# Layer 1's rational function from squares: ScalarE squares h, quotients of coefficients kept in registers, order table made anew

## The chip, the core and the metric

The kernel runs on one core of a Trainium2 chip. A core has five engines that run side by side, each through its own queue in order: TensorE (PE, matrix products into PSUM), VectorE (DVE), ScalarE (ACT), GpSimd (POOL) and SyncE (SP, which here only issues DMA transfers). The metric is the device time of one launch in microseconds. Three runs of the kernel before gave a median of 1600.95 us (1600.79 to 1603.09).

## What is computed

Attention with a packed set of 32 queries per head, then two layers over 4608 tokens of 512 features, each with 2048 hidden units. Cut to what matters:

```
p_packed = softmax(p k^T / 8) v                 # 8 batches x 8 heads, 32 packed rows, 576 positions
x = softmax(q p_packed^T / 8) p_packed          # 4608 x 512 after the heads are joined

h = x @ w_in                                    # layer 1
P = a[0] + a[1]*h + a[2]*h*h + a[3]*h*h*h
Q = 1 + |b[0]|*|h| + |b[1]|*h*h
x = (P / (Q + 1e-6)) @ w_out

h = x @ moe2_w_in                               # layer 2
out = (h * cos(h)) @ moe2_w_out
```

The weights are 64-bit numbers in memory; the kernel makes 32-bit ones of them on the chip. Each matrix product of the layers is made of three products of high and low parts.

## The kernel before

**Stages.** The attention works in 16 units (8 batches, two groups of four heads). A unit transposes k and q on PE in two pieces each (`trans`; ACT copies the piece out of PSUM, `copied`), makes scores, takes the exponential, transposes it (`turn_exp`, copied out by `exp_copied`: the long part by ACT, the short one by DVE, L839), multiplies with v (`pack`), scales (`packed`, DVE, L854), and so on to the second softmax, whose last step on DVE is `turn_back` (L900). Layer 1 works in 128 items: an item is 288 tokens by 256 hidden units (a tile of 128 partitions x 576 columns). Layer 2 works in 144 items of 512 tokens by 128 hidden units. Weights are converted in pieces (`w_exp` and `w_low` on ACT, `w_abs` L676 and `w_join` L686 on DVE, then `w_hi` on ACT and `w_lo` on POOL for some).

**An item of layer 1.** `front` (PE, L1054) makes h in PSUM with 12 matmuls of 288 columns. ACT makes |h| (`absolute`, L1183, into V), a3*h + a2 (`lin`, L1169, into T) and |b1|*|h| + |b0| (`slope`, L1186, into U). DVE makes the cubic by Horner's rule: `cubic` step 0, T*h (L1178), and step 1, (T + a1)*h (L1180). POOL makes U*V (`denom`, L1192), which is Q - 1. ACT takes 1/Q as exp(-ln Q): `log` (L1195) and `inverse` (L1199), into V. DVE divides both polynomials: `over` on U, (U + 1 + 1e-6)*V, and on T, (T + a0)*V (L1203), and makes one correction step, `ratio` (L1207), whose result is -P/Q. ACT rounds it to the high part (`upper`, L1235), DVE makes the low part (`lower`, L1238), and PE multiplies both with w_out into four accumulators (`back`, L1091, six matmuls each). When an accumulator is complete, `done1` (ACT, L1104) copies it out with the factor -1. The coefficients lie in `par`, one column each, read as per-partition pointers.

**Order and buffers.** The order of the work is written out by hand: every piece of work is a numbered step, and the table `ORDER` holds, for each engine, the numbers in the order in which they are issued. `Plan.order` merges the five lists and gives each tile its buffer. T has four buffers, U and V three each; h lies in one of two large PSUM buffers (`b2`), which the attention's transposed pieces and scores use too (`tr`); four smaller PSUM buffers serve as accumulators (`acc`), two of them, while the attention runs, as its small ones (`one`). A POOL pass that reads two tensors is held behind the DVE instruction issued before it.

Of the kernel before, what the change touches and what calls it, by code (L numbers as in the profile page):

```python
# [490 lines left out]
def pack_attention_moe_moe_kernel(  # L491
# [143 lines left out]
    def flat2(t):  # L635
        return t.rearrange("p a b -> p (a b)")
# [852 lines left out]
```

## Time and profile before

| | us |
|---|---|
| median of three runs | 1600.95 |
| profiled execution | 1599.52 |
| its span, first to last instruction | 1597.7 |
| PE busy in the span | 1546.3 |
| DVE busy | 1281.6 |
| ACT busy | 1028.1 |
| POOL busy | 343.0 |

The attention and the first conversions fill the time to about 100 us, then items of layer 1 run among the attention's last units and, from about 240 us, the second half of layer 1's weights; from about 320 us on layer 1 alone runs; at about 800 us layer 2 begins. A busy share is to be read by stretch, since the stages have different limits, and a chain of waits is to be read only where the bounding engine idles.

### The profile page before, as it was taken

How to read it: one execution, taken by the hardware profiler on the slowest of the kernel's cores; microseconds unless marked ns; L12 is line 12 of the kernel's file. 1: busy time of each engine (PE TensorE's matmuls, PEld its weight loads, DVE VectorE, ACT ScalarE, POOL GpSimd, SP SyncE). 2: the span in 40 equal slices, each digit the busy share in tenths (PEclk: the TensorE clock that was granted, in tenths of full speed). 3: DMA queues.
4: the chain of work that ended last, by engine and by line, in shares of the span. 5: the costliest groups of instructions: out<-in, count | busy, mean ns of one | idle time of the engine just before them, and what ended most of it. 6: DMA issues, size and time to landing. Idle time of an engine off the chain costs nothing.

```text
span 1597.7 us, 26582 instructions
## 1 busy us (share of the span) xinstructions
PE 1546.3 (97%) x10128; PEld 1337.7 (84%) x10128; DVE 1281.6 (80%) x2025; ACT 1028.1 (64%) x1747; POOL 343.0 (21%) x276
## 2 busy tenths in 40 slices
PE   6889998899999999999999999999999999999998
PEld 4567998799999998999888888888888888888887
DVE  4799999999999999999889866676666666666665
ACT  6899999999999898999776433333333333333332
POOL 1445442434343333333333100000000000000000
PEclk9999999999999999999999999999999999999999
DMA  9994215321221211122664211011010101020010
GB/s 299 322 310 144 81 50 179 126 62 53 80 81 61 66 65 55 51 80 77 236 195 139 60 40 46 21 40 40 14 33 16 39 0 34 7 60 8 7 27 27
DMA packets 98304, 133.01 MB, mean 83 GB/s; under 512 B 20865, under 2 KB 75137, under 8 KB 98177
## 3 DMA queue, kind: packets, MB, share of 16 engines
q1 hardware_dynamic: 97792, 130.79, 26.3%
q8 instruction: 80, 1.31, 0.3%
q10 hardware_dynamic: 384, 0.52, 0.1%
q14 instruction: 48, 0.39, 0.1%
HBM read 93.52 MB, written 37.75 MB: 82 GB/s over the span
## 4 chain that ended last, share of the span: by engine, by line
PE 77%; DVE 9%; ACT 6%; DMA 4%; issue 2%; POOL 1%; SPq 0%; DVEq 0%; ACTq 0%; POOLq 0%
PE acc L1091 42%; PE b L1070 24%; PE b L1054 9%; PE b L1004 2%; DMA raw<-in_moe_w_in_dram 1%; DVE U L1203 1%; DVE T L1203 1%; DVE T L1207 1%; DVE gl L1238 1%; DVE T L1178 1%; DVE T L1180 1%; ACT V L1183 1%; DVE sc L676 1%; ACT T L1169 1%; PE b L768 1%
## 5 line engine op out<-in xcount | busy, mean ns | idle before, releaser
L1091 PE MATMUL acc<-gh,wo 128*128 128x288 f32 x2048 | 420.7, 299 | 6.8 <-ACT ob L1104 6.2
L1091 PEld LDWEIGHTS acc<-gh,wo 128*128 128x128 f32 x2048 | 329.1, 189 | 31.8 <-issue 15.5
L1091 PE MATMUL acc<-wo,gh 128*128 128x512 f32 x1152 | 354.7, 389 | 0.0
L1091 PE MATMUL acc<-gl,wo 128*128 128x288 f32 x1024 | 302.8, 296 | 3.0 <-DVE gl L1238 3.0
L1192 POOL TENSOR_TENSOR U<-U,V 128x576 f32<-128x576 f32 x128 | 183.8, 1445 | 373.0 <-DVE T L1207 124.5
L1091 PEld LDWEIGHTS acc<-wo,gh 128*128 128x128 f32 x1152 | 216.2, 188 | 45.1 <-POOL wo L698 0.2
L1226 ACT ACTIVATE U<-U 128x512 f32<-128x512 f32 x144 | 90.9, 631 | 213.4 <-DVE U L1222 213.4
L1091 PE MATMUL acc<-wo,gl 128*128 128x512 f32 x576 | 224.1, 389 | 0.0
L1171 ACT ACTIVATE T<-b 128x512 f32<-128x512 f32 x144 | 85.8, 596 | 182.5 <-PE b L1070 182.3
L1091 PEld LDWEIGHTS acc<-gl,wo 128*128 128x128 f32 x1024 | 193.7, 189 | 4.0 <-DVE gl L1238 3.7
L1211 DVE TENSOR_SCALAR T<-T 128x512 f32<-128x512 f32 x144 | 62.9, 437 | 120.9 <-ACT T L1171 120.2
L1229 DVE TENSOR_TENSOR V<-U,b 128x512 f32<-128x512 f32 x144 | 98.6, 685 | 51.1 <-ACT U L1226 49.6
L1238 DVE TENSOR_TENSOR gl<-V,gh 128x512 fp32r<-128x512 f32 x144 | 99.1, 689 | 48.9 <-PE acc L1091 34.7
L1091 PEld LDWEIGHTS acc<-wo,gl 128*128 128x128 f32 x576 | 108.1, 188 | 22.3
L1235 ACT CAST gh<-V 128x512 fp32r<-128x512 f32 x144 | 87.9, 615 | 57.9 <-PE acc L1091 29.0
L1186 ACT ACTIVATE U<-V,par 128x576 f32<-128x576 f32 x128 | 111.0, 871 | 1.4 <-DVE T L1207 0.6
L1203 DVE SCALAR_TENSOR_TENSOR T<-T,par,V 128x576 f32<-128x576 f32 x128 | 106.6, 841 | 5.2 <-ACT V L1199 5.2
L1169 ACT ACTIVATE T<-b,par 128x576 f32<-128x576 f32 x128 | 105.9, 830 | 6.6 <-PE b L1054 3.5
L1180 DVE SCALAR_TENSOR_TENSOR T<-T,par,b 128x576 f32<-128x576 f32 x128 | 102.0, 809 | 6.1 <-ACT V L1183 3.5
L1218 DVE SCALAR_TENSOR_TENSOR U<-T,U 128x512 f32<-128x512 f32 x144 | 102.6, 712 | 3.0
L1238 DVE TENSOR_TENSOR gl<-T,gh 128x576 fp32r<-128x576 f32 x128 | 100.3, 788 | 4.4 <-ACT gh L1235 3.5
L1203 DVE SCALAR_TENSOR_TENSOR U<-U,V 128x576 f32<-128x576 f32 x128 | 99.6, 783 | 3.0 <-POOL U L1192 1.5
(184 smaller groups left out, 3071.7 us busy)
## 6 DMA issues: line engine op xcount, KB each, us to landing
raw<-in_moe_w_out_dram SPq DMA_DIRECT2D x32, 512.0 KB, 3.8
raw<-in_moe_w_in_dram SPq DMA_DIRECT2D x30, 512.0 KB, 4.5
x<-ob SPq DMA_DIRECT2D x24, 576.0 KB, 3.5
k_in<-in_k_dram SPq DMA_DIRECT2D x16, 576.0 KB, 7.0
q_in<-in_q_dram SPq DMA_DIRECT2D x16, 576.0 KB, 6.0
v_in<-in_v_dram SPq DMA_DIRECT2D x16, 512.0 KB, 7.0
w<-sc SPq DMA_DIRECT2D x32, 256.0 KB, 3.2
out_dram<-sc SPq DMA_DIRECT2D x102, 64.0 KB, 1.7
```

The lines of the kernel that those rows point to most:

```text
L1054: nc.tensor.matmul(TILE["h", j][:, e, 0:HS], lhsT=w[:, o : o + P], rhs=x[:, g, :], start=n == 0, stop=n == 3 * NG - 1,)
L1070: nc.tensor.matmul(h, lhsT=w[:, ks], rhs=x, start=n == 0, stop=n == 3 * KC - 1)
L1091: nc.tensor.matmul(o, lhsT=w, rhs=x, start=i == first and n == 0, stop=i == last and n == len(todo) - 1,)
L1169: nc.scalar.activation(T, hidden(j), AF.Identity, scale=par[:, 3:4], bias=par[:, 2:3])
L1180: nc.vector.scalar_tensor_tensor(T, T, par[:, 1:2], h, op0=ALU.add, op1=ALU.mult)
L1186: nc.scalar.activation(shaped(j, "U"), shaped(j, "V"), AF.Identity, scale=par[:, 5:6], bias=par[:, 4:5])
L1192: return nc.gpsimd.tensor_tensor(Q, Q, V, op=ALU.mult)
L1203: return nc.vector.scalar_tensor_tensor(t, t, add_, shaped(j, "V"), op0=ALU.add, op1=ALU.mult)
L1218: return nc.vector.scalar_tensor_tensor(Y, T, -C2, Y, op0=ALU.mult, op1=ALU.add)
L1226: nc.scalar.activation(Y, Y, AF.Sin, bias=PI/2)
L1229: nc.vector.tensor_tensor(shaped(j, "V"), shaped(j, "U"), hidden(j), op=ALU.mult)
L1238: return nc.vector.tensor_tensor(shaped(j, "gl"), result(j), shaped(j, "gh").bitcast(F32), op=ALU.subtract)
```

## The change

In layer 1 the polynomials are built from one square. ACT makes U = b0*|h| (`absolute`, with a scale) and V = (r*h)^2 with r the square root of |b1| (`square`); `lin` and `slope` go from layer 1. POOL adds them, U + V = Q - 1, in place of a product. DVE makes T = (h + a2/a3)*V (`cubic` step 0) and T = h*c + T (step 1), which is the cubic without its constant, up to a factor; `over` adds the constant. The factor is taken out at the end by `done1`. The quotients are made once, by five steps `coef`, into a tile of columns `cf`; three scales (for `absolute`, `square` and `done1`) are loaded into ACT's registers. In the attention, ACT instead of DVE copies the short part of the transposed exponential and makes `packed`, and the second pieces of the transposed k and q lie in the small PSUM buffers. The order table is made anew, since the steps' numbers shift; items, buffers and loads are the same in number.

```
@@ attention
     def piece(u, nm, j):
         t0, t1 = PIECES[j]
-        return flat2(TILE[nm + "ps", u, j])[:, 0 : (t1 - t0) * P]
+        ps = TILE[nm + "ps", u, j]
+        return (ps if j else flat2(ps))[:, 0 : (t1 - t0) * P]
...
-            nc.vector.tensor_copy(e1T[:D, 4, :], ps[:D, 0:P])
+            nc.scalar.copy(e1T[:D, 4, :], ps[:D, 0:P])
...
-        nc.vector.tensor_scalar(
+        nc.scalar.activation(
             TILE["pp", u],
             TILE["ppp", u][:, 0:D].unsqueeze(1).to_broadcast([P, 2, D]),
-            TILE["sm", u][:, 3:4],
-            None,
-            op0=ALU.mult,
+            AF.Copy,
+            scale=TILE["sm", u][:, 3:4],
         )
...
@@ layer 1
-        nc.scalar.mul(TILE["ob", c, a][:, m, :], TILE["acc", 0, c, a, m][:, 0:HS], -1.0)
+        nc.scalar.activation(TILE["ob", c, a][:, m, :], TILE["acc", 0, c, a, m][:, 0:HS], AF.Copy, scale=REG["out"])
...
-    def lin(j):
-        T = shaped(j, "T")
-        if layer(j) == 0:
-            nc.scalar.activation(T, hidden(j), AF.Identity, scale=par[:, 3:4], bias=par[:, 2:3])
...
+    def absolute(j):
+        nc.scalar.activation(shaped(j, "U"), hidden(j), AF.Abs, scale=REG["b0"])
+
+    def square(j):
+        nc.scalar.activation(shaped(j, "V"), hidden(j), AF.Square, scale=REG["root"])
+
+    def denom(j):
+        Q, V = shaped(j, "U"), shaped(j, "V")
+        return nc.gpsimd.tensor_tensor(Q, Q, V, op=ALU.add)
 
     def cubic(j, e):
         T, h = shaped(j, "T"), hidden(j)
         if e == 0:
-            nc.vector.tensor_tensor(T, T, h, op=ALU.mult)
+            nc.vector.scalar_tensor_tensor(T, h, cf[:, 17:18], shaped(j, "V"), op0=ALU.add, op1=ALU.mult)
         else:
-            nc.vector.scalar_tensor_tensor(T, T, par[:, 1:2], h, op0=ALU.add, op1=ALU.mult)
-
-    def absolute(j):
-        nc.scalar.activation(shaped(j, "V"), hidden(j), AF.Abs)
-
-    def slope(j):
+            nc.vector.scalar_tensor_tensor(T, h, cf[:, 19:20], T, op0=ALU.mult, op1=ALU.add)
...
-        t, add_ = shaped(j, "TU"[e]), (par[:, 0:1], ONE_EPS)[e]
+        t, add_ = shaped(j, "TU"[e]), (cf[:, 18:19], ONE_EPS)[e]
...
@@ the factors, once
-    def par_abs():
-        nc.scalar.activation(par[:, 4:6], par[:, 4:6], AF.Abs)
+    REG = {}
+
+    def coef(k):
...
+        if k == 0:
+            nc.scalar.activation(col(0, 6), par[:, 0:6], AF.Abs)
+        elif k == 1:
+            V.tensor_scalar(cf[:, 6:8], cf[:, 3:6:2], TINY, None, op0=ALU.max)
+        elif k == 2:
+            nc.scalar.activation(col(8), col(7), AF.Ln)
+            nc.scalar.activation(col(9), col(8), AF.Exp, scale=0.5)
+        elif k == 3:
+            V.reciprocal(col(10), col(9))
...
+        else:
+            for nm, a in (("b0", 4), ("root", 11), ("out", 20)):
+                REG[nm] = nc.scalar.alloc_register(nm)
+                nc.scalar.reg_load(REG[nm], cf[0:1, a : a + 1].bitcast(I32))
...
@@ the steps of an item
-        add("ACT", 545, key, absolute, j, tail=95, r=[("h", j)], new=[("V", ("V", j), *W2P)])
-        add("ACT", 730, key, lin, j, tail=100, r=[("h", j), ("par",)], new=[("T", ("T", j), *W2P)])
-        add("ACT", 760, key, slope, j, tail=105, r=[("V", j), ("par",)], new=[("U", ("U", j), *W2P)])
-        add("DVE", 665, key, cubic, j, 0, tail=85, r=[("h", j)], w=[("T", j)])
+        add("ACT", 545, key, absolute, j, tail=95, r=[("h", j), ("par",)], new=[("U", ("U", j), *W2P)])
+        add("ACT", 545, key, square, j, tail=95, r=[("h", j)], new=[("V", ("V", j), *W2P)])
         add("POOL", 1392, key, denom, j, tail=50, r=[("V", j)], w=[("U", j)])
+        add("DVE", 730, key, cubic, j, 0, tail=85, r=[("h", j), ("V", j)], new=[("T", ("T", j), *W2P)])
         add("DVE", 730, key, cubic, j, 1, tail=85, r=[("h", j)], w=[("T", j)])
```

## Rows read from the trace of the kernel before

**Rows 1.** The page's first section: busy us (share of the span), instructions.
```profile
PE 1546.3 (97%) x10128; PEld 1337.7 (84%) x10128; DVE 1281.6 (80%) x2025; ACT 1028.1 (64%) x1747; POOL 343.0 (21%) x276
```

**Rows 2.** Stretches: length, busy us per engine, granted clock, DMA share, GB/s.
```profile
0.00:100.00 100.00, 75.25 (x1105) 53.12 (x1105) 65.09 (x137) 76.85 (x154) 31.46 (x46) 0.95 0.97 311
100.00:320.00 220.00, 202.95 (x1847) 176.77 (x1840) 212.63 (x324) 204.26 (x350) 90.88 (x70) 1.00 0.41 133
320.00:760.00 440.00, 439.06 (x3427) 418.59 (x3426) 419.54 (x566) 406.85 (x654) 162.82 (x115) 1.00 0.21 67
760.00:820.00 60.00, 55.73 (x358) 51.76 (x357) 49.54 (x74) 45.71 (x78) 21.25 (x16) 0.97 0.69 228
820.00:1597.70 777.70, 773.35 (x3405) 637.44 (x3403) 534.78 (x928) 294.41 (x515) 36.57 (x30) 1.00 0.14 38
```

**Rows 3.** Timeline of PE at 502 us: start, length, engine, line, operation.
```profile
502.23 0.29 PE L1091 MATMUL acc<-gl,wo 128*128 128x288 f32 x1
502.36 0.43 PE L1091 MATMUL acc<-gh,wo 128*128 128x288 f32 x2
502.63 0.29 PE L1091 MATMUL acc<-gl,wo 128*128 128x288 f32 x1
```

**Rows 4.** PE's waits, 320 to 760 us: total us, times, longest.
```profile
PE b L1054 <- DVE T L1180: 0.6, 2, 0.3
PE acc L1091 <- ACT ob L1104: 0.4, 1, 0.4
```

**Rows 5.** Timeline of DVE at 96 us and at 320 us.
```profile
95.94 0.75 DVE L1238 TENSOR_TENSOR gl<-T,gh 128x576 fp32r<-128x576 f32 x1
...
319.81 0.68 DVE L676 SCALAR_TENSOR_TENSOR sc<-sc,sc 128x512 uint32<-128x512 uint32 x1
320.41 0.75 DVE L1238 TENSOR_TENSOR gl<-T,gh 128x576 fp32r<-128x576 f32 x1
321.08 0.68 DVE L686 SCALAR_TENSOR_TENSOR sc<-raw,sc 128x512 uint32<-128x512 uint32 x1
321.68 0.74 DVE L1238 TENSOR_TENSOR gl<-T,gh 128x576 fp32r<-128x576 f32 x1
```

**Rows 6.** Groups of instructions on ACT: busy us, mean ns, idle before.
```profile
L1186 ACT ACTIVATE U<-V,par 128x576 f32<-128x576 f32 x128 | 111.0, 871 | 1.4 <-DVE T L1207 0.6
L1169 ACT ACTIVATE T<-b,par 128x576 f32<-128x576 f32 x128 | 105.9, 830 | 6.6 <-PE b L1054 3.5 <-DVE gl L1238 2.4
L1183 ACT ACTIVATE V<-b 128x576 f32<-128x576 f32 x128 | 82.9, 647 | 11.1 <-PE b L1054 6.6 <-DVE T L1180 2.0 <-DVE T L1178 1.6
L1226 ACT ACT_TABLE_LOAD x1 | 1.3, 1283 | 0.0
```

**Rows 7.** Groups of instructions on DVE, the same columns.
```profile
L1180 DVE SCALAR_TENSOR_TENSOR T<-T,par,b 128x576 f32<-128x576 f32 x128 | 102.0, 809 | 6.1 <-ACT V L1183 3.5
L1178 DVE TENSOR_TENSOR T<-T,b 128x576 f32<-128x576 f32 x128 | 94.1, 746 | 8.7 <-ACT T L1169 5.4 <-ACT V L1183 2.6
L854 DVE TENSOR_SCALAR pp<-one,sm 128x128 f32<-128x128 f32 x16 | 5.2, 328 | 3.2 <-PE one L845 3.2
L839 DVE COPY e1T<-one 64x128 f32<-64x128 f32 x16 | 4.3, 267 | 5.4 <-PE one L832 5.4
L824 DVE RECIPROCAL sm<-sm 128x1 f32<-128x1 f32 x16 | 2.6, 164 | 0.5
```

**Rows 8.** DVE's longest waits, 100 to 340 us: total us, times, longest.
```profile
DVE sc L676 <- ACT sc L670: 2.0, 2, 1.1
DVE T L1178 <- ACT T L1169: 1.8, 4, 1.0
DVE sm L807 <- PE b L795: 1.5, 1, 1.5
DVE T L1180 <- ACT V L1183: 1.0, 2, 0.8
DVE m01l L1017 <- ACT m01h L1013: 0.9, 2, 0.6
```

**Rows 9.** PE's longest wait, 760 to 830 us.
```profile
PE acc L1091 <- DVE gl L1238: 3.0, 3, 1.5
```

**Rows 10.** Stretch 790 to 800 us, columns as in rows 2.
```profile
790.00:800.00 10.00, 8.31 (x47) 7.84 (x48) 7.10 (x11) 4.02 (x7) 2.71 (x3) 0.83 0.70 227
```

More of the change, by code (lines that the diff above doesn't have):

```diff
@@ L535, in pack_attention_moe_moe_kernel @@
     EARLY = 8
+    TINY = 2.0**-60
     CE = 8
@@ L629, in pack_attention_moe_moe_kernel @@
     par = POOL["cp"].tile([P, 8], F32, name="par")
+    cf = POOL["cp"].tile([P, 24], F32, name="cf")
     cst = POOL["cp"].tile([P, 4], F32, name="cst")
@@ L934, in transposed @@
                 home = [] if j else [(nm + "T", (nm + "T", u), [P, NT9 * P], F32)]
-                go("PE", 125 * (t1 - t0), trans, nm, j, tail=200, r=[(nm, u)], new=[("tr", (nm + "ps", u, j), *ps2), *home])
+                go("PE", 125 * (t1 - t0), trans, nm, j, tail=200, r=[(nm, u)], new=[("one", (nm + "ps", u, j), *ps1) if j else ("tr", (nm + "ps", u, j), *ps2), *home])
                 go("ACT", 50 + int(107 * (t1 - t0)), copied, nm, j, tail=100, r=[(nm + "ps", u, j)], w=[(nm + "T", u)])
@@ L945, in attention @@
             go("PE", (560, 160)[a], turn_exp, a, tail=200, r=[("e1", u)], new=[("one", ("e1t", u, a), *ps1), *home])
-            go(*(("DVE", 190) if a else ("ACT", 480)), exp_copied, a, tail=90, r=[("e1t", u, a)], w=[("e1T", u)])
+            go("ACT", 170 if a else 480, exp_copied, a, tail=90, r=[("e1t", u, a)], w=[("e1T", u)])
         transposed("q")
         go("PE", 840, pack, tail=230, r=[("e1T", u), ("v", u)], new=[("one", ("ppp", u), *ps1), ("pp", ("pp", u), [P, 2, D], F32)])
-        go("DVE", 270, packed, tail=70, r=[("ppp", u), ("sm", u)], w=[("pp", u)])
+        go("ACT", 270, packed, tail=70, r=[("ppp", u), ("sm", u)], w=[("pp", u)])
         go("PE", 160, turned, "pp", tail=150, r=[("pp", u)], new=[("one", ("ppt", u), *ps1), ("lhpp", ("lhpp", u), [P, P], F32)])
@@ L1164, in hidden @@
         return TILE["h", j][:, :, 0:HS] if layer(j) == 0 else TILE["h", j][:, 0, :]
-    def lin(j):
-        T = shaped(j, "T")
-        if layer(j) == 0:
-            nc.scalar.activation(T, hidden(j), AF.Identity, scale=par[:, 3:4], bias=par[:, 2:3])
-        else:
-            nc.scalar.activation(
-                T, hidden(j), AF.Identity, scale=1.0 / (2 * PI), bias=0.25
-            )
+    def absolute(j):
[5 more added lines that the diff above has]
+        return nc.gpsimd.tensor_tensor(Q, Q, V, op=ALU.add)
     def cubic(j, e):
@@ L1177, in cubic, with lin @@
         if e == 0:
-            nc.vector.tensor_tensor(T, T, h, op=ALU.mult)
+            nc.vector.scalar_tensor_tensor(T, h, cf[:, 17:18], shaped(j, "V"), op0=ALU.add, op1=ALU.mult)
         else:
-            nc.vector.scalar_tensor_tensor(T, T, par[:, 1:2], h, op0=ALU.add, op1=ALU.mult)
-    def absolute(j):
-        nc.scalar.activation(shaped(j, "V"), hidden(j), AF.Abs)
-    def slope(j):
+            nc.vector.scalar_tensor_tensor(T, h, cf[:, 19:20], T, op0=ALU.mult, op1=ALU.add)
+    def lin(j):
         nc.scalar.activation(
-            shaped(j, "U"), shaped(j, "V"), AF.Identity, scale=par[:, 5:6], bias=par[:, 4:5]
+            shaped(j, "T"), hidden(j), AF.Identity, scale=1.0 / (2 * PI), bias=0.25
         )
-    def denom(j):
-        Q, V = shaped(j, "U"), shaped(j, "V")
-        return nc.gpsimd.tensor_tensor(Q, Q, V, op=ALU.mult)
     def log(j):
@@ L1265, in par_load, with col @@
         nc.sync.dma_start(par[:, 4:6], rat_b.unsqueeze(0).to_broadcast([P, 2]))
-    def par_abs():
-        nc.scalar.activation(par[:, 4:6], par[:, 4:6], AF.Abs)
+    REG = {}
+    def coef(k):
+        def col(a, n=1):
+            return cf[:, a : a + n]
+        V = nc.vector
+        if k == 0:
[7 more added lines that the diff above has]
+            V.reciprocal(col(10), col(9))
+            V.scalar_tensor_tensor(col(11), col(10), col(7), col(9), op0=ALU.mult, op1=ALU.add)
+            V.tensor_scalar(col(11), col(11), 0.5, None, op0=ALU.mult)
+            V.scalar_tensor_tensor(
+                col(12).bitcast(U32), par[:, 3:4].bitcast(U32), 0x80000000, col(6).bitcast(U32), op0=ALU.bitwise_and, op1=ALU.bitwise_or
+            )
+            V.tensor_tensor(col(13), col(11), col(11), op=ALU.mult)
+            V.reciprocal(col(14, 2), col(12, 2))
+            V.tensor_tensor(col(16), col(13), col(14), op=ALU.mult)
+            V.tensor_tensor(col(17), par[:, 2:3], col(14), op=ALU.mult)
+            V.tensor_scalar(col(18, 2), par[:, 0:2], col(16), None, op0=ALU.mult)
+            V.scalar_tensor_tensor(col(20), col(12), -1.0, col(15), op0=ALU.mult, op1=ALU.mult)
+        else:
+            for nm, a in (("b0", 4), ("root", 11), ("out", 20)):
+                REG[nm] = nc.scalar.alloc_register(nm)
+                nc.scalar.reg_load(REG[nm], cf[0:1, a : a + 1].bitcast(I32))
     add("SP", 960, ("v", 0, -20), par_load, w=[("par in",)], bus=300)
-    add("ACT", 60, ("v", 0, 0), par_abs, tail=100, r=[("par in",)], w=[("par",)])
+    for n in range(5):
+        add(("ACT", "DVE")[n % 2], (60, 80, 200, 900, 900)[n], ("v", 0, 0), coef, n, tail=100, r=[("par in",)], w=[("par",)])
     for u in range(NU):
```

598 rows, old and new, of the table ORDER are left out of this document.

## Prediction

> **What bounds the kernel now.** Read the page's first section first: TensorE (PE) is busy for 97% of the span [rows 1]. That share mixes stages, so the next view is the table of stretches [rows 2]. From 820 us to the end (layer 2) PE is busy 773 of 778 us. From 320 to 760 us (layer 1 in its steady state) it is busy 439 of 440 us. A busy PE need not be a PE at its peak, so the timeline comes next: three matmuls of 288 columns start every 0.40 us, 133 ns each, without a hole [rows 3]. An item of layer 1 has 36 of them (12 in `front`, 24 in the four `back`), so PE alone needs 36 x 0.1333 = 4.80 us for it. PE's own waits over those 440 us sum to 1.0 us [rows 4]. In both long stretches nothing that another engine does faster can be worth anything.
>
> What is left are the places where PE idles [rows 2]: 24.8 us before 100 us, 17.1 us from 100 to 320 us, 4.3 us from 760 to 820 us. In the first the DMA engines are 97% busy at 311 GB/s with attention inputs and weights. In the second VectorE (DVE) is busy 212.6 of 220 us, ScalarE (ACT) 204.3, PE 203.0: DVE is the nearest to full, ACT just behind. Here the attention's last units, the late half of layer 1's weights and the first 34 items share the engines. The 34th `lower` on DVE (item 33) starts at 321.7 us, the first (item 0) at 95.9 us [rows 5], and right behind that 34th one PE stops idling. So the time is what DVE needs to bring item 33 to PE, plus what PE has left from there; the second part is fixed at PE's own pace.
>
> **The change part by part.** ACT, layer 1. `slope` goes (871 ns), `lin` (830 ns, two pointer operands) becomes `square`, which like `absolute` reads h from PSUM; `absolute` takes 647 ns [rows 6]. What ACT pays for a scale held in a register no row shows: bounds are 0 and the 183 ns that two pointers cost `lin` over `absolute`; I take 0, the nearest form being `absolute` itself, with an immediate scale. So 871 + 183 = 1.05 us fall off ACT per item, 135 us over 128 items, or 88 us at the dear bound. In PE's steady stretch this is worth nothing: ACT's load falls under a bound that it does not set.
>
> DVE, layer 1. `cubic` step 0 turns from a plain product (746 ns) into an add-and-multiply with a pointer (like step 1, 809 ns) [rows 7]: +63 ns per item, 8.1 us over 128 items. In the steady stretch DVE has 440 - 419.5 = 20.5 us idle [rows 2] to cover it there (92 x 63 ns = 5.8 us); if that cover were gone it would cost those 5.8 us.
>
> Attention. Per unit one copy of 267 ns and one scaling of 328 ns go from DVE to ACT [rows 7], 9.5 us over 16 units; ACT pays about the same, taken at DVE's price. The second piece of each transposed k and q goes to the one-bank PSUM pool, so the two large buffers that layer 1 shares come free sooner. Two units of the 16 read their q late among layer 1's items; the rest lies in the stretch that the DMA fills. I cost this piece at nothing, between -2 us (PE's holes there that end on ACT) and +2 us (the small pool becoming the tight one).
>
> Factors. Eleven instructions of one to two columns on DVE, at 164 ns a reciprocal [rows 7] about 1.8 us, three small passes on ACT and three register loads from SBUF. No row shows a register load; the bounds are 0 and some 2 us each, which is more than anything the page shows of the sequencers. They stand among the first 18 entries of ACT's table, ahead of a conversion pass and the copies of unit 0's q. Until 100 us ACT idles 23.2 us and DVE 34.9 us [rows 2], and the DMA sets the pace, so 0. Without that cover the first items would come up to 6 us later.
>
> Order. Counting the entries of both tables of DVE up to item 0's `lower` and on to item 33's gives 112 and 428 before, 94 and 394 after: between the two points 316 entries become 300. The 16: five copies and six scalings of the attention (-3.3 us), two `w_join`, one `w_abs` and one `cubic` step put behind item 33 (-2 x 0.68 - 0.68 - 0.81 = -2.9 us [rows 5, 7]), one `turn_back` put ahead of item 0 (about -0.8 us). Against it 33 x 63 ns = +2.1 us. Sum -4.9 us; neighbours on DVE overlap by about 0.07 us (an instruction of 0.68 us is followed after 0.60 [rows 5]), so 16 entries fewer are worth 1.1 us less: -4 us. The entries put off come back behind item 33, where PE is the bound.
>
> DVE's idle time in this stretch is 7.4 us [rows 2]. Of its five longest named waits, up to 340 us, four are on ACT, 2.0 + 1.8 + 1.0 + 0.9 = 5.7 us, and one on PE [rows 8]. ACT loses, up to item 33's `upper`, 35 `slope` and 36 x 183 ns = 37 us and takes some 10 us of attention: 27 us of the 281 that it has worked by then. I take half of DVE's idle time as won, -3.7 us, with bounds 0 and -5.7.
>
> Transition to layer 2. PE idles 4.3 us between 760 and 820 us [rows 2], 3.0 us of it waiting for `lower` on DVE [rows 9], which is fed by ACT and DMA; the granted clock is 0.83 in one slice there, a part of it at 1.2 in place of 2.4 GHz after PE had idled [rows 10]. With ACT lighter and the loads of x and the weights standing earlier in SP's table I take half, -2.1 us, bounds 0 and -4.3.
>
> Sum: -4 - 3.7 - 2.1 = -9.8 us. The profiled execution took 1599.5 us (span 1597.7 and 1.8 around it), so 1589.7; the median of the runs is 1.4 us above that execution: **1591 us**. Own range, from the bounds of the terms (-4 - 5.7 - 4.3 - 2 and -4 + 2): 1585 to 1599.
>
> **The rivals.** (a) *Deep gain*: ACT was the second limit from 100 to 320 us, and its queue delays DVE also where no wait is listed. Then PE loses its holes of both stretches but a few: 17.1 + 4.3 = 21.4 us, 1579 us. For it: three engines at 92 to 97% at once, so each must have cost the others something. Against: DVE's work alone fills 97% of the stretch. Chance 0.16.
>
> (b) *Given back*: the items come earlier, but PE's start is set by the loads, and the steady stretch, with 63 ns more per item on DVE and `absolute` now holding a U buffer (three of them) until `ratio`, loses its closeness to 100%. 5.8 us of DVE work there and holes of 3 to 4 us, about 1600 us. For it: 311 GB/s in the first 100 us [rows 2]; against: 20.5 us of idle DVE. Chance 0.15.
>
> (c) *Slower, a new wait*: `log` overwrites V, which `cubic` step 0 on DVE now reads, so ACT's `log` waits for DVE; behind it in ACT's queue stand `upper` of older items, which PE waits for. ACT gains 1.05 us per item and idled (220 - 204.3) / 33 = 0.48 us per item from 100 to 320 us. From a wait of 1.5 us per item on, ACT is slower than before and the bound: at 1.7 us, 33 x 0.2 = 6.6 us, 1608 us. For it: DVE's queue is 97% full. Against: in the new table a median of five DVE entries (some 3.5 us) stands between `cubic` step 0 and the first `over` of an item, and of five ACT entries between `square` and `log`. Chance 0.09.
>
> (d) *Slower, table loads*: if `square` were not in the table that holds `log` and `inverse`, each item would load a table twice; the load that the trace shows took 1283 ns [rows 6]. 256 x 1.28 = 328 us on ACT, whose work up to 820 us (733 less about 125) would pass 930 us: some 1720 us. For it nothing in the trace; against it that Abs, Identity, Ln and Exp alternate with no load between. Chance 0.02. The Trainium skill (ScalarE: Activation LUTs, Table sets: the hidden batching unit) says that relu, copy, identity and abs fill every set and names exp and ln for this one; square it does not name there. The trace agrees for abs and identity, and cannot tell for square; by the list taken as whole the time would be these 1720 us, by the rows 1591.
>
> **How the numbers follow.** Forecast 0.55, (a) 0.16, (b) 0.15, (c) 0.09, (d) 0.02; 0.03 for what I don't see, shared. What this measurement can tell from no change is 0.2%, 3.2 us: faster ends at 1597.7, slower begins at 1604.2. The forecast is faster but for its last 1 us: faster 0.55 + 0.16 = 0.71, same 0.16, slower 0.13. The range leaves out (d), the far part of (c), and what lies beyond the full worth of (a): 1579 to 1605.
>
> **What would show it.** In the profile after: ACT's busy time some 125 us lower; DVE's within 5 us of 1282; item 33's `lower` near 313 us instead of 321.7; PE still at 133 ns per matmul, and its steady stretch beginning earlier by as much as the end comes earlier; DVE's waits on ACT in the stretch halved. Wrong would be: an unchanged time of item 33's `lower` (then the loads set the start), DVE busy under 95% there (a new wait), table loads among the items, or `square` above 830 ns.

## The result and the profile after

The changed kernel takes 1615.0 us (median of four runs, 1612.4 to 1616.2) against 1600.9 us for the kernel before beside it: ratio 1.0083, 95% interval 1.0066 to 1.0101. It is slower by 0.8%, where 1591 us and a range of 1579 to 1605 us had been forecast. The profiled execution took 1615.28 us, its span is 1613.5 us.

The first section of the page after (busy us, share of the span, instructions; before it is [rows 1]):

```profile
PE 1564.4 (97%) x10128; PEld 1337.4 (83%) x10128; DVE 1280.6 (79%) x2004; ACT 921.1 (57%) x1653; POOL 344.1 (21%) x276
```

ACT is busy 107 us less, DVE the same. TensorE is busy 18.1 us *more*, with the same 10128 matmuls. The stretches tell where (columns as in [rows 2]; the last row runs to the end of this span):

```profile
100.00:320.00 220.00, 202.74 (x1871) 179.57 (x1864) 213.67 (x314) 179.05 (x331) 93.34 (x72) 0.99 0.43 136
320.00:760.00 440.00, 438.52 (x3433) 418.60 (x3432) 425.87 (x570) 330.89 (x568) 162.06 (x116) 1.00 0.23 73
760.00:820.00 60.00, 56.38 (x362) 51.60 (x361) 50.93 (x76) 39.64 (x71) 21.83 (x16) 1.00 0.59 194
...
820.00:1613.50 793.50, 789.24 (x3390) 635.76 (x3388) 529.72 (x922) 293.53 (x512) 35.32 (x29) 1.00 0.13 37
```

In the three stretches from 100 to 820 us PE's busy time lies within 0.7 us of [rows 2]. In layer 2, whose code the change doesn't touch, PE's busy time over its recorded matmuls was 773.35 / 3405 = 0.2271 us each before and is 789.24 / 3390 = 0.2328 us after. The granted clock is 1.00 in both, so it isn't the clock. Nor is it a wait: PE's named waits after 830 us sum to 0.2 us. The matmuls themselves follow each other more slowly. (Of a matmul's two operands one is loaded first, `lhsT` in the kernel, and the other, `rhs`, streams past it. In `front` of layer 2 the weights s are loaded and a or x streams; in its `back` gh or gl is loaded and the weights wo stream.) Two views of them, first the timeline of PE in layer 2 after (start, length, engine, line, operation), with three matmuls of a `back` every 0.70 us:

```profile
1000.20 0.63 PE L1087 MATMUL acc<-wo,gh 128*128 128x512 f32 x2
1000.67 0.39 PE L1087 MATMUL acc<-wo,gl 128*128 128x512 f32 x1
1000.90 0.63 PE L1087 MATMUL acc<-wo,gh 128*128 128x512 f32 x2
1001.37 0.39 PE L1087 MATMUL acc<-wo,gl 128*128 128x512 f32 x1
1001.60 0.63 PE L1087 MATMUL acc<-wo,gh 128*128 128x512 f32 x2
```

and the same view of the kernel before, with three every 0.68 us:

```profile
1002.38 0.61 PE L1091 MATMUL acc<-wo,gh 128*128 128x512 f32 x2
1002.83 0.39 PE L1091 MATMUL acc<-wo,gl 128*128 128x512 f32 x1
1003.05 0.61 PE L1091 MATMUL acc<-wo,gh 128*128 128x512 f32 x2
1003.51 0.39 PE L1091 MATMUL acc<-wo,gl 128*128 128x512 f32 x1
1003.74 0.61 PE L1091 MATMUL acc<-wo,gh 128*128 128x512 f32 x2
```

So 233 ns per matmul instead of 227. The shortest, the median and the longest duration of each group say that all of a group are slower, not a few (matmuls overlap, so a duration holds a part of the next). Before, by tile, from 860 to 1560 us:

```profile
L1091 PE MATMUL acc<-wo,gh x1024: 387/389/401, 859.7 to 1556.9; 128*128 128x512 f32 x171
...
L1070 PE MATMUL b<-a,s x240: 387/389/412, 893.4 to 1448.1; 128*128 128x512 f32 x120
...
L1070 PE MATMUL b<-x,s x240: 387/389/494, 974.5 to 1538.1; 128*128 128x512 f32 x120
```

and after:

```profile
L1087 PE MATMUL acc<-wo,gh x1000: 392/396/403, 861.4 to 1556.3; 128*128 128x512 f32 x167
...
L1066 PE MATMUL b<-a,s x240: 387/389/398, 889.4 to 1460.9; 128*128 128x512 f32 x120
...
L1066 PE MATMUL b<-x,s x240: 391/396/400, 975.0 to 1552.3; 128*128 128x512 f32 x120
```

The last pair is the clue. A `front` matmul that takes a tile named a beside the weights s is as fast as before (389), one that takes x beside the same weights is not (396). The instruction is the same; only the tile differs.

What a and s share is the side of SBUF from which their pools are laid out. Weights, a, T, U and V stand in pools on the left, packed upward one after the other; x, ob, gh and gl in pools on the right, packed downward. Every tile of the two layers after the first pool has a size that is a multiple of 256 bytes per partition, and in the compiled program before each of them begins at 192 modulo 256, on both sides. The change adds one small tile ahead of all others on the left:

```
     par = POOL["cp"].tile([P, 8], F32, name="par")
+    cf = POOL["cp"].tile([P, 24], F32, name="cf")
```

24 columns are 96 bytes, so those on the left move from 192 to 288, which is 32 modulo 256; those on the right stay at 192. That is a part of the change which the prediction did not weigh at all.

### The profile page after: what moved, and what is told of

Same layout as the page of the kernel before. It is cut to its first block, busy times and chain, and to the rows that moved or that the text cites. A ratio compares the mean times of both kernels' runs of the same rounds, so it can differ in the third digit from the quotient of the medians.

```text
span 1613.5 us, 26523 instructions
## 1 busy us (share of the span) xinstructions
PE 1564.4 (97%) x10128; PEld 1337.4 (83%) x10128; DVE 1280.6 (79%) x2004; ACT 921.1 (57%) x1653; POOL 344.1 (21%) x276
## 4 chain that ended last, share of the span: by engine, by line
PE 79%; DVE 8%; ACT 5%; DMA 4%; issue 2%; POOL 1%; SPq 0%; DVEq 0%; ACTq 0%; POOLq 0%
PE acc L1087 43%; PE b L1066 24%; PE b L1050 10%; PE b L1000 1%; DMA q_in<-in_q_dram 1%; DVE T L1197 1%; DMA raw<-in_moe_w_in_dram 1%; DVE U L1193 1%; DVE T L1177 1%; DVE T L1193 1%; DVE T L1175 1%; DVE gl L1228 1%; DMA raw<-in_moe_w_out_dram 1%; DVE sc L672 1%; DMA p_in<-in_p_dram 0%
## 5 line engine op out<-in xcount | busy, mean ns | idle before, releaser
L1087 PE MATMUL acc<-wo,gh 128*128 128x512 f32 x1152 | 363.1, 396 | 0.0
L1219 DVE TENSOR_TENSOR V<-U,b 128x512 f32<-128x512 f32 x144 | 98.6, 685 | 56.7 <-ACT U L1216 55.4
L1175 DVE SCALAR_TENSOR_TENSOR T<-b,cf,V 128x576 f32<-128x576 f32 x128 | 102.5, 810 | 11.2 <-ACT U L1163 7.3
L1193 DVE SCALAR_TENSOR_TENSOR T<-T,cf,V 128x576 f32<-128x576 f32 x128 | 107.5, 844 | 3.5 <-ACT V L1189 3.2
L1185 ACT ACTIVATE V<-U 128x576 f32<-128x576 f32 x128 | 87.5, 685 | 37.0 <-POOL U L1170 28.8
L1228 DVE TENSOR_TENSOR gl<-T,gh 128x576 fp32r<-128x576 f32 x128 | 104.3, 817 | 3.9 <-ACT gh L1225 3.0
L1177 DVE SCALAR_TENSOR_TENSOR T<-b,cf,T 128x576 f32<-128x576 f32 x128 | 100.9, 810 | 2.7 <-ACT U L1163 0.9
L1163 ACT ACTIVATE U<-b 128x576 f32<-128x576 f32 x128 | 83.3, 651 | 33.5 <-DVE T L1197 16.0
```

Source lines behind the costliest of these rows:

```text
L1087: nc.tensor.matmul(o, lhsT=w, rhs=x, start=i == first and n == 0, stop=i == last and n == len(todo) - 1,)
L1175: nc.vector.scalar_tensor_tensor(T, h, cf[:, 17:18], shaped(j, "V"), op0=ALU.add, op1=ALU.mult)
L1177: nc.vector.scalar_tensor_tensor(T, h, cf[:, 19:20], T, op0=ALU.mult, op1=ALU.add)
L1193: return nc.vector.scalar_tensor_tensor(t, t, add_, shaped(j, "V"), op0=ALU.add, op1=ALU.mult)
L1219: nc.vector.tensor_tensor(shaped(j, "V"), shaped(j, "U"), hidden(j), op=ALU.mult)
L1228: return nc.vector.tensor_tensor(shaped(j, "gl"), result(j), shaped(j, "gh").bitcast(F32), op=ALU.subtract)
```

## The experiments

**Moving tiles and nothing else.** The theory: the new tile's 96 bytes cost layer 2 its pace, by the places of the operands. The rival: something that the change does, such as its order or what DVE and ACT do beside PE, slows the matmuls. Four kernels. The first is the kernel before with an unused tile of 96 bytes in the place of `cf`:

```
     par = POOL["cp"].tile([P, 8], F32, name="par")
+    POOL["cp"].tile([P, 24], F32, name="gap")
```

> The kernel before, with an unused tile of 96 bytes per partition where the change puts cf; nothing else differs. Theory 1 (addresses): the change's loss is that its 96-byte tile moves the tiles allocated after it from a multiple of 64 bytes to 32 beyond one, and the 512-column matmuls of layer 2 then start every 233 ns instead of 227: about 3400 x 6 ns = 20 us at most, so 1614 to 1620 us with no algebra changed, layer 1 as before. Rival (order): the new order table or the new arithmetic slows layer 2; then this is 1601 us with matmuls at 227 ns.

1620.0 us, ratio 1.0114 [1.0094, 1.0134]. Its stretch of layer 2:

```profile
820.00:1590.00 770.00, 769.85 (x3308) 620.70 (x3307) 521.58 (x905) 289.48 (x506) 37.93 (x31) 1.00 0.13 37
```

0.2327 us per matmul. An unused tile alone brings the whole loss, and no instruction of the change is in this kernel. This settles it between the two theories. The next three ask how fine the grid is. The changed kernel with 128 bytes for `cf`:

```
-    cf = POOL["cp"].tile([P, 24], F32, name="cf")
+    cf = POOL["cp"].tile([P, 32], F32, name="cf")
```

> The kernel after, with cf 32 columns wide (128 bytes) instead of 24, so that all later tiles lie at multiples of 64 bytes again; nothing else differs. Theory 1 (addresses): matmuls of layer 2 back at 227 ns, and what the change does besides shows alone: about 1597 us, since layer 1 ended 3.6 us earlier in the kernel after. Rival (order): 1615 us as the kernel after, 233 ns.

1612.2 us, 1.0065 [1.0048, 1.0082], hardly better:

```profile
820.00:1590.00 770.00, 770.00 (x3318) 622.98 (x3317) 519.66 (x905) 289.59 (x505) 36.71 (x30) 1.00 0.13 38
```

0.2321 us. The kernel before with a gap of 64 bytes:

```
+    POOL["cp"].tile([P, 16], F32, name="gap")
```

> The kernel before with an unused tile of 64 bytes in the same place: tiles keep their place relative to 64 bytes but change it relative to 128. Theory 1 with a grain of 64 bytes: 1601 us and 227 ns. Theory 1 with a grain of 128 bytes: above 1610 us. Rival (order): 1601 us.

1610.9 us, 1.0052 [1.0032, 1.0073], 0.2312 us per matmul (770.00 / 3331). And the kernel before with the *right* side moved down by 32 bytes instead, by the edge tile that lies there first:

```
-    POOL["edge"].tile([P, 8], F32, name="edge")
+    POOL["edge"].tile([P, 16], F32, name="edge")
```

> The kernel before with 32 bytes more in the unused tile at the other end of SBUF: x, ob, gh and gl move to 32 beyond a multiple of 64 bytes, weights, T, U, V stay. If what counts is that the two operands of a matmul differ in their place relative to 64 bytes: all of layer 2's matmuls with x, ob or gh, gl slow to about 233 ns, 1612 to 1618 us. If what counts is the place of the weights' side alone: 1601 us, 227 ns. Rival (order): 1601 us.

1617.6 us, 1.0098 [1.0076, 1.0121], 0.2322 us (769.84 / 3316). So either side may be moved, and it is the difference that costs. My guess of a grid of 64 bytes fell with the second and the third: 64 and 128 bytes cost nearly as much as 96.

**The grid, and which operands.** If the grid is 256 bytes, a `cf` of 256 bytes gives the pace back, and with it shows what the change is worth by itself:

```
-    cf = POOL["cp"].tile([P, 24], F32, name="cf")
+    cf = POOL["cp"].tile([P, 64], F32, name="cf")
```

> The kernel after, with cf 64 columns wide (256 bytes). Every tile again starts at the same place relative to 256 bytes as every other one, as in the kernel before (192 beyond a multiple), which 96, 128 and 64 bytes did not give. Theory (common place relative to 256 bytes): layer 2's matmuls at 227 ns; the kernel after is 5.0 us faster than the kernel before with the same 96-byte shift (1615.0 against 1620.0), so 1601.3 - 5 = 1596 us. Rival (the exact addresses of the kernel before, or another cause in the change): 1612 us or more, 231 to 233 ns.

1594.1 us (1593.2 to 1598.6), ratio 0.9957 [0.9945, 0.9969]: faster than both kernels. Layer 2 runs at 0.2272 us (766.90 / 3376):

```profile
820.00:1591.00 771.00, 766.90 (x3376) 631.49 (x3374) 525.96 (x916) 290.76 (x507) 34.56 (x29) 1.00 0.14 38
```

Next, both sides of the kernel before moved by 128 bytes, so that all tiles of the layers begin at 64 modulo 256:

```
-    POOL["edge"].tile([P, 8], F32, name="edge")
+    POOL["edge"].tile([P, 40], F32, name="edge")
...
+    POOL["cp"].tile([P, 32], F32, name="gap")
```

> The kernel before, with 128 bytes more unused at both ends of SBUF: all tiles at 64 beyond a multiple of 256 instead of 192, all still alike. Theory (common place): 1601 us, 227 ns. Rival (the place itself counts): 1610 us or more, 231 ns or more.

1601.0 us, 0.9996 [0.9983, 1.0009], 0.2271 us (769.58 / 3389). The place itself doesn't matter; that the tiles agree does.

Then single groups of tiles, each moved by 32 bytes with gaps of 32 bytes ahead and, where other tiles follow, 224 behind, so that all others keep their place modulo 256. First T, U and V, on which only DVE, ACT and POOL work:

```
+    POOL["ep"].tile([P, 8], F32, name="gap0")
...
+    POOL["ld"].tile([P, 56], F32, name="gap1")
...
+        POOL["sr"].tile([P, 56], F32, name="gap2")
```

> The kernel before with T, U and V alone, which only VectorE, ScalarE and GpSimd touch, moved by 32 bytes. If TensorE's pace suffers from their accesses at another place than its own: 230 ns or more, above 1608 us. If it is a matter of a matmul's own operands: 227 ns, 1601 us, within 3 us for what VectorE itself may lose.

1600.6 us, 0.9992 [0.9982, 1.0002], 0.2270 us (769.77 / 3391). Nothing, so it's not the other engines' operands. Then only the weights of `back`, wo:

```
+    POOL["wo0"].tile([P, 8], F32, name="gap0")
+    POOL["sl2"].tile([P, 56], F32, name="gap1")
...
+        POOL["wo1"].tile([P, 8], F32, name="gap2")
```

> The kernel before with the w_out tiles alone moved by 32 bytes (other tiles by whole multiples of 256). If it is the two operands of the same matmul that must lie alike: the back products of layer 2 (half of its matmuls, wo against gh and gl) slow to 233 ns, the front products stay at 227: about 1728 x 6 ns = 10 us, 1611 us. If it is tiles of VectorE and ScalarE against those of TensorE, or any shift: no change, 1601 us, or both halves slow, above 1615 us.

1614.6 us, 1.0081 [1.0058, 1.0104]. By tile (the view of min, median and max from above):

```profile
L1093 PE MATMUL acc<-wo,gh x1012: 393/395/399, 860.3 to 1557.5; 128*128 128x512 f32 x169
...
L1072 PE MATMUL b<-a,s x240: 387/389/398, 895.7 to 1460.4; 128*128 128x512 f32 x120
L1072 PE MATMUL b<-x,s x240: 387/389/448, 978.1 to 1552.1; 128*128 128x512 f32 x120
```

The `back` matmuls, whose operand was moved, are slow; those of `front`, with both operands in place, are fast in the median, x among them. The complement, the weights of `front` alone:

```
+    POOL["sl"].tile([P, 8], F32, name="gap0")
+    POOL["wo0"].tile([P, 56], F32, name="gap1")
+    POOL["sl2"].tile([P, 8], F32, name="gap2")
+    POOL["a2p"].tile([P, 56], F32, name="gap3")
...
+        POOL["sr"].tile([P, 8], F32, name="gap4")
...
+            if nm == "wo1":
+                POOL[nm].tile([P, 56], F32, name="gap5")
```

> The kernel before, with only the tiles that hold the weights of `front` (both layers) 32 bytes further on; the weights of `back`, x, gh, gl and all others stay. Theory A (the pace of a 512-column matmul goes by the places of its own two operands, modulo 256 bytes): the front matmuls of layer 2 that take x0 or x1 slow down from 227 to 230 to 234 ns, the back ones stay at 227, and the time is 3 to 8 us over that of the kernel before, the complement of the 12.4 us that moving the weights of `back` alone cost. Theory B (it is any difference between TensorE's tiles, whichever matmul runs): both slow down, 13 to 19 us. Theory C (only back's operands matter, since back has most of the matmuls): no change.

1611.4 us, 1.0070 [1.0049, 1.0092]:

```profile
L1095 PE MATMUL acc<-wo,gh x1011: 387/389/398, 859.7 to 1559.8; 128*128 128x512 f32 x169
...
L1074 PE MATMUL b<-a,s x240: 389/395/413, 892.7 to 1455.7; 128*128 128x512 f32 x120
...
L1074 PE MATMUL b<-x,s x240: 389/395/416, 975.0 to 1546.9; 128*128 128x512 f32 x120
```

Now `front` is slow with every tile that it takes, a too, and `back` is fast. The theory's kind of outcome came, its size did not: I had put 3 to 8 us, since I counted only the matmuls that take x, and it is 11.

**What the change is worth by itself.** With the pace out of the way, three kernels ask where its gain comes from. They are read by the start of `lower` on DVE: for item 0, item 33, the first item of layer 2 and the last. For the kernel before [rows 5] has the first two, and the others are

```profile
816.63 0.69 DVE L1238 TENSOR_TENSOR gl<-V,gh 128x512 fp32r<-128x512 f32 x1
...
1588.27 0.69 DVE L1238 TENSOR_TENSOR gl<-V,gh 128x512 fp32r<-128x512 f32 x1 [0.44 <-PE acc L1091]
```

The rows of the changed kernel:

```profile
98.56 0.75 DVE L1228 TENSOR_TENSOR gl<-T,gh 128x576 fp32r<-128x576 f32 x1
...
319.05 0.74 DVE L1228 TENSOR_TENSOR gl<-T,gh 128x576 fp32r<-128x576 f32 x1
...
813.03 0.68 DVE L1228 TENSOR_TENSOR gl<-V,gh 128x512 fp32r<-128x512 f32 x1
...
1603.96 0.69 DVE L1228 TENSOR_TENSOR gl<-V,gh 128x512 fp32r<-128x512 f32 x1 [0.89 <-PE acc L1087]
```

and of the one with 256 bytes:

```profile
96.01 0.75 DVE L1228 TENSOR_TENSOR gl<-T,gh 128x576 fp32r<-128x576 f32 x1
...
316.00 0.75 DVE L1228 TENSOR_TENSOR gl<-T,gh 128x576 fp32r<-128x576 f32 x1
...
809.85 0.68 DVE L1228 TENSOR_TENSOR gl<-V,gh 128x512 fp32r<-128x512 f32 x1
...
1582.06 0.69 DVE L1228 TENSOR_TENSOR gl<-V,gh 128x512 fp32r<-128x512 f32 x1 [0.76 <-ACT gh L1225]
```

The differences of these starts, read the same way in each kernel:

| kernel | item 0 starts | item 0 to 33 | item 33 to layer 2 | layer 2, first to last item |
|---|---|---|---|---|
| before | 95.9 | 225.7 | 494.9 | 771.6 |
| before, gap of 96 bytes | 97.7 | 226.9 | 494.2 | 790.8 |
| changed | 98.6 | 220.5 | 494.0 | 790.9 |
| changed, 256 bytes | 96.0 | 220.0 | 493.8 | 772.2 |
| and `square` twice | 98.7 | 227.0 | 514.0 | 772.0 |
| and plain `cubic` step 0 | 97.5 | 220.7 | 493.0 | 772.1 |
| before, short `slope` | 98.6 | 224.4 | 493.8 | 771.5 |

Where the tiles agree layer 2 takes 771.5 to 772.2 us, where they lie 96 bytes apart 791; the change adds or takes nothing there. The change itself is worth 5.7 us between item 0 and item 33 (6.4 between the two rows with 96 bytes) and 1.1 or 0.2 us up to layer 2. How far to trust this the kernels that only move tiles show. Over all eight traces with the old code the way from item 0 to item 33 takes 224.2 to 227.5 us, over the three of the changed code and the one with plain `cubic` 220.0 to 222.6; from there to layer 2 it is 493.3 to 495.0 and 493.0 to 494.0. So the gain up to item 33 is clear, some 5 us, and the one behind it isn't; a difference of 2 us between two single traces says nothing. Item 0's own start spreads more, from 94.7 to 100.0 us over the old code.

First, ACT's relief taken back in part, in the kernel with 256 bytes:

```
         nc.scalar.activation(shaped(j, "V"), hidden(j), AF.Square, scale=REG["root"])
+        nc.scalar.activation(shaped(j, "V"), hidden(j), AF.Square, scale=REG["root"])
```

> The changed kernel with 256 bytes for the new tile (all operands at one place again), and `square` issued twice: 650 ns go back on ACT per item, 62% of the 1.05 us that the change took off, nothing else is altered. Without it that kernel stood at 0.9957 of the kernel before. Theory A (the gain before item 33 comes from ACT's lighter load, which shortens the waits of DVE on ACT): most of the 5.7 us at item 33 goes, its lower starts at 319 to 322 us, the time is 1597 to 1601. Theory B (the gain comes from what DVE no longer does ahead of item 33; ACT's load sets nothing): item 33 stays at 316 us within 1 us, the time within 2 us of 1594, ratio 0.995 to 0.997.

1623.8 us, 1.0152 [1.0132, 1.0173]. Worse than both theories: 7.0 us up to item 33, about what theory A expects, and 20 us more in the stretch that I had called PE's own. Its steady stretch and its longest waits of DVE and of PE there (total us, times, longest):

```profile
320.00:760.00 440.00, 427.76 (x3297) 401.80 (x3295) 405.83 (x544) 368.30 (x630) 158.39 (x113) 1.00 0.21 66
```

```profile
DVE T L1176 <- ACT U L1163: 15.0, 18, 1.5
DVE T L1176 <- ACT V L1167: 10.9, 13, 1.8
```

```profile
PE b L1050 <- DVE T L1178: 6.3, 12, 1.3
```

ACT is busy 368 of 440 us, less than the 407 of [rows 2], and yet it now holds up DVE, and DVE holds up PE. How full an engine is does not say whether it is late: the second `square` stands in each item between h and the first step of the cubic, in an order that was laid out without it.

Second, the dearer form of `cubic` step 0 taken back in the same kernel:

```
-            nc.vector.scalar_tensor_tensor(T, h, cf[:, 17:18], shaped(j, "V"), op0=ALU.add, op1=ALU.mult)
+            nc.vector.tensor_tensor(T, shaped(j, "V"), h, op=ALU.mult)
```

> The changed kernel with 256 bytes for the new tile, and `cubic` step 0 as a plain product of h and V, as in the kernel before; the coefficient that the pointer brought is left out, so another polynomial is computed. It prices the 63 ns per item that DVE pays for the pointer. Theory A (DVE's work sets the pace from 100 to 320 us): 34 x 63 ns = 2.1 us earlier at item 33, 314 us, and the time 2 us lower, some 1592. Theory B (DVE also waits for others there, so its work is covered): item 33 at 316 us, the time unchanged, 1594. Rival to both, steady stretch: if DVE's 63 ns there cost PE something, the time falls by more, up to 8 us.

1593.8 us, 0.9951 [0.9934, 0.9968], against 0.9957 [0.9945, 0.9969] with the pointer; 220.7 us from item 0 to item 33 against 220.0. The product took 745 ns in place of 810. That is what theory B expects, and the 8 us of the rival are out; the 2 us of theory A lie within the spread of the times and of these traces, so they are not excluded.

Third, relief of ACT in the kernel before and in its order:

```
-            shaped(j, "U"), shaped(j, "V"), AF.Identity, scale=par[:, 5:6], bias=par[:, 4:5]
+            shaped(j, "U")[:, :, 0:16], shaped(j, "V")[:, :, 0:16], AF.Identity, scale=par[:, 5:6], bias=par[:, 4:5]
...
-        return nc.gpsimd.tensor_tensor(Q, Q, V, op=ALU.mult)
+        return nc.gpsimd.tensor_tensor(Q, V, V, op=ALU.mult)
```

> The kernel before with its own order, but `slope` on ACT takes 16 of 144 columns of each half instead of all, and `denom` on POOL multiplies V by V; so the linear factor of the denominator is left out and another quotient is computed. POOL, DVE and PE keep every instruction and its size. ACT loses an estimated 0.6 us per item, 77 us in layer 1, more than half of the 1.05 us per item of the change, and nothing else changes. From item 0's lower to item 33's the kernel before takes 225.8 us, the changed kernel with all operands at one place 220.0. Theory A (ACT's load itself set a part of the pace there): that stretch falls to 221 to 223 us and the time with it, 1595 to 1598. Theory B (the gain needs the new order, which takes entries off DVE; the old order hides the old load of ACT): the stretch stays within 1.5 us of 225.8 and the time within 2 us of the kernel before, ratio 0.9985 to 1.0015.

1597.6 us, 0.9972 [0.9959, 0.9985]. (I wrote 144 columns for a half; a half has 288.) Two groups of this kernel, to be read against 871 ns for `slope` in [rows 6] and 1445 ns for `denom` before:

```profile
L1186 ACT ACTIVATE U<-V,par 128x32 f32<-128x32 f32 x128 | 52.2, 412 | 2.7 <-DVE T L1207 1.9
```

```profile
L1192 POOL TENSOR_TENSOR U<-V 128x576 f32<-128x576 f32 x128 | 145.7, 1147 | 401.4 <-DVE T L1207 143.3 <-DVE gl L1238 45.4 <-DVE U L1203 41.2
```

ACT lost 0.46 us per item, but `denom`, which now reads one tile twice, lost 0.30 us on POOL too. So this kernel relieves two engines, not ACT alone as the expectation had it. The result lies between the two theories: the time falls by 2.4 to 6.6 us, which A expects, while the trace shows 1.3 us up to item 33 and 1.2 behind it, both within the spread of the old code. So the lighter ACT and POOL together are worth some 2 to 7 us in the old order, and which of the two brings it is not shown. Nor is it shown how the changed kernel's 7 us split between the lighter ACT and the new order with its fewer entries on DVE: no run has the new order with the old load of ACT in its old place. The kernel with `square` twice shows only that the new order doesn't bear 0.65 us more of ACT between h and the cubic.

## Why the prediction was wrong

**The step that failed** is "the second part is fixed at PE's own pace", put for all that follows item 33 and priced at 0 for layer 2. It measured +19.3 us (771.6 to 790.9). PE does run at its own pace there, without waits, as the prediction said; but the pace is no constant of the instruction. [rows 3] had shown 133 ns for the 288-column matmul of layer 1, and I carried "PE's own pace" over to layer 2, whose matmuls have 512 columns and were not looked at one by one. In layer 1 the change left it alone (133 ns after as before); in layer 2 it went from 227 to 233 ns. And the list of the change's parts held instructions, buffers and the order, but not the one new tile's size, since a tile of 96 bytes issues nothing.

**The other terms**, read where the tiles agree (the table above), had the right sign and were too large. The forecast was -4 - 3.7 = -7.7 us up to item 33; it is -5.7, or some -5 over all traces. The longest waits of DVE that were to vanish did so in part: after, from 100 to 340 us, against [rows 8],

```profile
DVE T L1175 <- ACT U L1163: 1.5, 4, 0.5
DVE T L1175 <- ACT V L1166: 1.5, 2, 1.2
DVE U L1193 <- ACT V L1189: 1.1, 1, 1.1
DVE sc L672 <- ACT sc L666: 0.9, 2, 0.7
```

four waits on ACT, 5.0 us in place of 5.7. The first two have taken the place of the wait for `lin` in [rows 8]: the first step of the cubic now waits for `absolute` and `square`, which stand together ahead of it. DVE's idle time from 100 to 320 us fell from 7.4 to 6.3 us (220 - 213.67), not by half. The transition to layer 2 was put at -2.1 us, half of PE's idle time there; PE's wait for `lower` fell from 3.0 [rows 9] to 2.3 us, its idle time from 760 to 820 us from 4.3 to 3.6 (60 - 56.38), and from item 33 to layer 2 the change took off 0.2 to 1.1 us. By its time the kernel with 256 bytes gained 6.9 us (a ratio of 0.9957) in place of 9.8, and at 1594.1 us it lies in the range of 1579 to 1605 that the changed kernel missed.

**The prices** held. `absolute` with its scale in a register takes 651 ns and `square` 650, in place of the 647 of [rows 6]; a scale from a register costs some 4 ns at most. `cubic` step 0 takes 810 ns, as its form does in [rows 7]. After, on ACT and DVE (busy us, mean ns):

```profile
L1185 ACT ACTIVATE V<-U 128x576 f32<-128x576 f32 x128 | 87.5, 685 | 37.0 <-POOL U L1170 28.8 <-DVE T L1177 4.9 <-DVE mx L888 1.4
...
L1163 ACT ACTIVATE U<-b 128x576 f32<-128x576 f32 x128 | 83.3, 651 | 33.5 <-DVE T L1197 16.0 <-PE b L1050 15.1 <-DVE T L1175 1.3
L1166 ACT ACTIVATE V<-b 128x576 f32<-128x576 f32 x128 | 82.8, 650 | 23.0 <-PE b L1050 21.5 <-DVE U L1193 0.9 <-DVE T L1193 0.2
...
L1463 ACT ACT_TABLE_LOAD x1 | 1.3, 1283 | 0.7 <-PEq L1492 0.7
```

```profile
L1228 DVE TENSOR_TENSOR gl<-T,gh 128x576 fp32r<-128x576 f32 x128 | 104.3, 817 | 3.9 <-ACT gh L1225 3.0 <-PE acc L1087 0.9
L1175 DVE SCALAR_TENSOR_TENSOR T<-b,cf,V 128x576 f32<-128x576 f32 x128 | 102.5, 810 | 11.2 <-ACT U L1163 7.3 <-ACT V L1166 3.4
```

ACT's busy time fell by 107 us, where 125 were forecast from sums of durations: the page counts overlapped neighbours once, and summed one by one ACT's durations fell by 123 us. Of the 8.1 us that the pointer adds on DVE the plain `cubic` step gave back at most the 2 us that no run here can tell from nothing. DVE's `lower` of layer 1 went from 788 to 817 ns with no edit of its own, in the kernel with 256 bytes too; in the kernels before with only a gap or with T, U and V moved it is 797 to 798. Why is open.

**The rivals.** (d), table loads, is out: two loads in the whole execution, as before, so `square` loads none. (c), `log` waiting for `cubic`, names a wait that did come but is small: before, `log` waited for POOL alone; now (L1185 above) it waits 4.9 us for the cubic's second step over all 128 items (and 1.2 us for the first, the one that the prediction named), and layer 1 became faster, not slower. (a), 1579 us, and (b), 1600 us, both lie below the 1615 measured. With 256 bytes the time, 1594, is nearest to the forecast's 1591, and (b)'s loss in the steady stretch did not come: PE is busy 438.5 of its 440 us after, 439.1 before. None of the rivals was the tile's place. What the kernel with `square` twice shows bears on (b): 0.65 us more of ACT per item does break the steady stretch in this order (PE busy 427.8 of 440 us). So "in PE's steady stretch this is worth nothing" holds within the spread for taking work off ACT (-0.2 to -1.1 us), not for putting it back.

## What to carry to other kernels

When a stage that an edit doesn't touch changes its time, and PE has no waits there, compare the start-to-start time of one form of matmul in both traces; if it differs at the same granted clock, compare where the tiles lie. A new small tile, a scratch column or a dropped buffer moves everything behind it, so pad small tiles to 256 bytes, or (not tried here) give them a pool of their own behind the large ones, so that the two operands of a matmul begin at the same place modulo 256 bytes: here that is 1.3% of the time (1615.0 against 1594.1 us) for 160 bytes. And a busy share tells whether an engine can be the bound by its work, not whether its next result comes in time.

## What the runs showed of the hardware

A 512-column matmul starts every 227 ns when its two operands begin at the same place modulo 256 bytes of their partition, and every 230 to 234 ns, by kernel and tile, when they don't; 32, 64, 96 and 128 bytes of difference all cost (0.2322, 0.2312, 0.2327 and 0.2321 us as a mean over layer 2), 0 and 256 don't (0.2271, 0.2272), and a common shift of 128 doesn't (0.2271). The effect follows the matmul whose operand was moved, and not the tiles on which only DVE, ACT and POOL work. The 288-column matmuls of layer 1 keep their 133 ns either way.

The Trainium skill (TensorE: Matmul & The Clock Gate, Step-by-step: what each phase is for) says that PE reads the streamed operand and the weights to be loaded through two independent ports, and that loading the next weights takes nothing from the running matmul. It names no place of the operands; if the two reads never touched each other, the kernel with only wo moved should have taken the 1602 us of the kernel before, and it took 1614.6. Where they meet no run here shows: it wasn't tried whether the load of the weights or the stream is the one that waits. The trace of the kernel with the weights of `front` moved has a hint. From the start of one `back` matmul to that of the next it is 227 ns, but from the last `back` matmul to a first `front` one, whose weights lie 32 bytes off, 234 (110 cases), though the `back` matmul's own two operands agree; and from a last `front` to a first `back` 233. So a matmul's neighbour counts beside its own pair. Three more rows say the same. With 128 bytes in `cf`, `front` matmuls with a and s, which had moved together, took 392 ns in the mean against 389 before; in the changed kernel those with raw (a tile on the left, too) and s took 393; and with only wo moved those with x and s took 392 against 390. So the place of a matmul's own two operands is the main part of the rule, and not all of it; the rest is open.
